# Order of the closing work: a stage's last operations, the copy-out of an accumulator and a gate's product, in a fused long-convolution and feed-forward kernel

## The chip, the cores and the metric

The kernel runs on one core of one Trainium2 chip. Its time is the device time of one execution in microseconds (us). Three runs of the kernel before gave 3606.44, 3606.97 and 3608.32 us; the median, 3606.97 us, is the number to compare with. All data are float32.

A core has five engines with a queue of instructions each, which they work off in order: TensorE (PE in the profile) for matmuls, VectorE (DVE), ScalarE (ACT), GpSimd (POOL), and SyncE (SP), which issues the transfers. Results of matmuls land in eight PSUM banks of 128 x 512 values, and a bank can be written again only when the engines that read it are done.

## The reference

Two blocks follow each other. The first is a long convolution along the sequence, by FFT, gated on both sides; its output, 49,920 rows of 128 values, is the input of a feed-forward block whose gate is a cosine.

```python
h_filt = (np.maximum(pos_emb @ w1, 0.0) @ w2) * np.exp(-0.01 * pos)[:, None]
u = x * v                                     # (4, 12480, 128)
y = irfft(rfft(u, n=2*S, axis=1) * rfft(h_filt, n=2*S, axis=0), n=2*S, axis=1)[:, :S]
a = (x * y).reshape(49920, 128)
h = a @ w_in                                  # 128 -> 2048
out = (h * np.cos(h)) @ w_out                 # 2048 -> 128
```

## The kernel before

**The convolution** is a two-level transform made of matmuls, one sequence (batch) b of the four after the other. Its stages are generators: `u_units` (multiply x and v, and fold), `f1_units` and `f2_units` (forward transform, and in the second the product with the filter's spectrum), `i1_units` and `i2_units` (inverse). Each of them is a call of `units` (L609), which cuts the n units of a stage into `parts` chunks each and yields after every chunk, with a number: what the chunk is worth in steps of the feed-forward block. Within a chunk it issues the matmuls of unit j, one piece of `after(j-1)` (what takes the previous unit out of PSUM) and one piece of the loads ahead. When the last unit's chunks are through, its own `after` is still to come: L632 issues all of it without a yield, and L634 yields `REST`, 3.0.

`after` has these pieces: in `u_units` two products of x and v (L441) and one pair of sums (L451); in `f1_units` one copy (L471); in `f2_units` four, each with one product of a PSUM bank and the spectrum on VectorE (L516, L518), every second one with a sum on GpSimd (L519); in `i1_units` two (a ScalarE copy and two VectorE sums, L563, L565); in `i2_units` the gating product (L591), after which `made` counts a finished group of 104 rows.

`inverse_units` (L815) runs `i2_units` of batch b and, between its chunks, the `u_units` of batch b+1, then the rest of these alone; it multiplies the chunk's worth of the `i2` by 3.5/1.5 (b = 0) or 3.4/1.5.

**The feed-forward block** takes blocks of 128 rows x 4 positions (512 tokens), n = 0 to 97, and each in 16 steps c of 128 of the 2048 hidden columns. A loop (L1203) with a running number i issues one step per turn, in this order:

1. `moe_down` of step i-7 (`LAG` = 7): 12 matmuls into the accumulator `acca` or 16 into `accb` (L911), in pairs of steps. On the block's last two steps `moe_evict` copies the accumulators out into `ot`: after pc = 14 L925 and L926 read `acca`; after pc = 15 the VectorE operations L929, L931 and L932 read `accb`. Because of the lag this falls on c = 5 and c = 6 of the next block. After pc = 15 comes one call of `convolve` (L1210).
2. `moe_up` of step i: four matmuls into a bank `ph` (L139), then L879 on ScalarE and L880 on VectorE, which bring the phase into one turn.
3. `act(i-1)`: `moe_act` of the step before, the sine on ScalarE (L885) and the product gate = h * cos(h) on VectorE (L886), the last reader of that step's bank.
4. `moe_sums` of the pair that began at i-4, on GpSimd (L894, L897, L898), which the later `moe_down` reads.
5. `convolve` (L1253), unless the next step is one with pc = 15 (`later`, L1251): then the chunk waits for step 1 of the next turn and stands behind the copy-out.

`convolve` (L1155) adds 1.0 to `owed` and takes chunks until their worth has used it up. Where rows are needed that no chunk has made yet, `load` (L1135) takes chunks without counting, and `hurry` (L1140) does so some steps earlier, up to the end of a stage, which it knows by a yield equal to `REST`.

`phase_bank` (L869) takes the bank of a step's phase from a pool of three (`ph`); once the convolution is through (`made` = 120) odd steps use the three banks (`cv`) that the convolution had. `accb` and `acca` have one bank each.

Ahead of the loop the filter's and the first sequence's transform run without the feed-forward block, with the same `units`.

Of the kernel before, what the change touches and what calls it, by code (L numbers as in the profile page):

```python
# [34 lines left out]
def kernel(  # L35
# [48 lines left out]
    B, S, D = x.shape  # L84
# [3 lines left out]
    R = S // N2  # L88
# [15 lines left out]
    NFC = DFF // P  # L104
    G = BANK // D
    UA = 2
    NG = N2 // G
# [3 lines left out]
    LAG = 7  # L111
# [487 lines left out]
        yield  # L599

    rows_psum = []
    made = [0]
    ot_tiles = []
    zbs = {}

# [3 lines left out]
    def units(n, steps, before, mm, after, parts, ahead=2, skip=0):  # L609


        for j in range(min(ahead, n)):
            for _ in before(j) or ():
                pass
        yield 0.0
        last = iter(())
        for j in range(n):
            early = iter(before(j + ahead) or () if j + ahead < n else ())
            now = None
            for i in range(parts):  # L620
                if i == skip or 2 * (i - skip) == max(parts, 2):
                    now = mm(j, now, int(i > skip))
                if i == 0 and parts == 1:
                    now = mm(j, now, 1)
                next(last, None)
                next(early, None)
                yield steps / parts
            for _ in early:
                pass
            next(last, None)  # L630
            last = after(j, now)
        for _ in last:  # L632
            pass
        yield REST  # L634

    SOME = range(2, NG, 5)
    REST = 3.0
# [207 lines left out]
    def first_row(n):  # L845
        return min(R + (n - 1) * P, NROWS) if n else 0
# [36 lines left out]

    def moe_act(ph, part, scale):
        nc.scalar.activation(part, part, AF.Sin, scale=scale)  # L885
        nc.vector.tensor_tensor(part, ph, part, op=ALU.mult)  # L886

    def moe_sums(pool, n, gt):
# [74 lines left out]
    with tc.manual_schedule():  # L963
        with tc.tile_pool(name="psum", bufs=8, space=PSUM) as psum, \
# [8 lines left out]
            parts = slots[:, :, 0:2 * N1, :].rearrange("p b (r k) i -> p r k b i", r=2)  # L973
# [158 lines left out]
        conv = convolutions()  # L1132
# [6 lines left out]

        def hurry(n):  # L1140

            while made[0] * R < first_row(n + 1):
                if next(conv) == REST:
                    return

        while made[0] == 0:
            next(conv)
# [3 lines left out]
        steps = [(n, c) for n in range(NALL) for c in range(NFC)]  # L1151
        hidden, pairs, gates, ots, obs = {}, {}, {}, {}, {}
        due, turned, taken = False, -3, {}

        def convolve():  # L1155
            nonlocal owed
# [7 lines left out]

            return taken[i] and not (taken[i - 1] and taken[i - 2])

        def act(i):
            if i in hidden:
                moe_act(*hidden.pop(i))

        def turns(n):

# [30 lines left out]
        for i in range(len(steps) + LAG):  # L1203
            if i >= LAG:
                pn, pc = steps[i - LAG]
                moe_down(pn, pc // 2, pc % 2, *gates[i - LAG - pc % 2])
                if pc >= NFC - 2:
                    ots[pn] = moe_evict(mpool, pn, pc % 2, ots.get(pn))
                if pc == NFC - 1:
                    convolve()  # L1210
            rest, early = iter(()), False
            if i < len(steps):
                n, c = steps[i]
                if c == 0:
                    due = 0 < n < SINGLE or n % 2
                if n == 0 and c == NFC // 2:
                    load(1)
                soon = n + 2 <= SINGLE or n % 2 == 0
                if c == (NFC - 5 if soon else SOON - 3) and 0 < n < NALL - 2:
                    hurry(n + 2)  # L1220
                if soon and c == (NFC - 2 if n else NFC - 1) and n + 2 < NALL:
                    load(n + 2)
                if n >= SINGLE and n % 2 and c == SOON and n + 2 < NALL:
                    load(n + 2)
                if n == 0 and c == NFC - 2:
                    pt = bank()
                    moe_turn(1, pt)
                    moe_turned(mpool, 1, pt)
                early = due and c >= AT
                if early:  # L1230
                    if n >= SINGLE:
                        act(i - 1)
                    convolve()
                    if n < SINGLE or c == AT + 3 or not just_taken(i):
                        due, turned = False, i
                        rest = turns(n)
                        next(rest)
                ph = phase_bank(c)
                next(rest, None)
                if c % 2 == 0:  # L1240
                    pairs[i] = mpool.tile([P, 2, BANK], F32, name="gt", bufs=4)
                hidden[i] = moe_up(mpool, n, c, pairs[i - c % 2], ph)
            for _ in rest:
                pass
            act(i - 1)
            if i - 4 in pairs:
                gates[i - 4] = moe_sums(mpool, steps[i - 4][0], pairs.pop(i - 4))
            if i == turned + 2:
                for k in sorted(obs):
                    moe_store(k, obs.pop(k))  # L1250
            later = i + 1 >= LAG and steps[i + 1 - LAG:][:1] and steps[i + 1 - LAG][1] == NFC - 1  # L1251
            if not early and not later:
                convolve()  # L1253
        for n in sorted(ots):
            moe_store(n, moe_rows(n, ots[n], moe_back(n, ots[n])))
# [28 lines left out]
```

## Time and profile before

| | |
|---|---|
| runs | 3606.44, 3606.97, 3608.32 us |
| profiled execution | 3609.1 us, of which the profile's span is 3607.3 us |
| mean granted TensorE clock | 0.999 |
| TensorE busy | 3554.6 us (99%) |
| VectorE busy | 2833.4 us (79%) |
| GpSimd busy | 2746.1 us (76%) |
| ScalarE busy | 2232.6 us (62%) |
| before the loop | to about 345 us of the span |
| convolution beside the feed-forward block | to about 2947 us |
| feed-forward block alone | from there to the end |

A row of the timeline gives the start, the duration, the engine, the line, the operation, what it writes and reads, and how many instructions were merged into it; in brackets stands how long the engine had been idle and what released it. A row of the stretches gives the length of the stretch and then each engine's busy time with its number of instructions, the granted clock of TensorE (1.00 is full speed), the share of time of the DMA engines and what they moved. A row of the waits says who waited for whom: total, times, longest. Matmuls overlap in the array, and their ends are modelled, so a short stop of TensorE can hide inside a "busy" duration; it shows between the starts of two rows.

### The profile page before, as it was taken

Reading aid. Unit: us, or ns where it says so; the run is one execution under the profiler, and the core shown is the slowest. Engines: PE = TensorE matmul, PEld = TensorE weight load, DVE = VectorE, ACT = ScalarE, POOL = GpSimd, SP = SyncE. Lnnn points to the kernel's source line nnn. Section 1 sums busy time; section 2 is a strip of 40 time slices with the busy share of each in tenths; the row PEclk is TensorE's granted clock in tenths of the full one; section 3 lists DMA queues with packets and bytes.
Section 4 is the critical chain, followed back from the end, with each engine's and each line's share of the span. In section 5 each row is a group of like instructions: output and inputs, shape, how many; then the busy total and the mean of one; then the engine's idle time right before and its main releaser. Section 6 shows DMA issues by size and latency. Waiting matters only on the chain.

```text
span 3607.3 us, 102214 instructions
## 1 busy us (share of the span) xinstructions
PE 3554.6 (99%) x40830; PEld 2549.7 (71%) x40830; DVE 2833.4 (79%) x5293; ACT 2232.6 (62%) x4482; POOL 2746.1 (76%) x3236
## 2 busy tenths in 40 slices
PE   8999999999999999999999999999999999999999
PEld 7996767666677777666677776766667876666666
DVE  7888885688887875688877786688887667877877
ACT  7776766656655556666655556665555456667666
POOL 7777985688856996688864897589884458888887
PEclk9999999999999999999999999999999999999999
DMA  7545540122214650022212661022220440000000
GB/s 191 157 147 169 159 117 13 34 72 72 70 32 127 173 139 17 24 76 72 75 30 60 172 171 51 13 64 70 75 63 20 132 125 25 16 22 25 16 22 17
DMA packets 224195, 281.84 MB, mean 78 GB/s; under 512 B 23386, under 2 KB 161122, under 8 KB 223594
## 3 DMA queue, kind: packets, MB, share of 16 engines
q1 hardware_dynamic: 223722, 275.30, 26.7%
q8 instruction: 325, 5.32, 0.6%
q14 instruction: 148, 1.21, 0.1%
HBM read 194.75 MB, written 80.46 MB: 76 GB/s over the span
## 4 chain that ended last, share of the span: by engine, by line
PE 82%; DVE 5%; POOL 2%; ACT 1%; issue 1%; DMA 1%; SPq 0%; ACTq 0%; DVEq 0%; POOLq 0%
PE ph L139 30%; PE accb L911 17%; PE cv L139 17%; PE acca L911 13%; PE cv L459 3%; DVE gt L886 2%; DVE gt L880 1%; PE cv L143 1%; PE ph L143 1%; ACT gt L879 1%; POOL ts L894 1%; DVE xt L441 0%; POOL ts L897 0%; DMA tm<-td 0%; DVE t L518 0%
## 5 line engine op out<-in xcount | busy, mean ns | idle before, releaser
L879 ACT ACTIVATE gt<-ph 128x512 int32<-128x512 f32 (+1 forms) x1376 | 822.0, 597 | 1138.6 <-PE ph L139 1100.0
L880 DVE SCALAR_TENSOR_TENSOR gt<-ph,gt 128x512 f32<-128x512 f32 (+1 forms) x1376 | 946.2, 688 | 658.7 <-ACT gt L879 654.9
L139 PE MATMUL ph<-at,w_in_sb 128*64 128x512 f32 (+2 forms) x5504 | 1424.8, 593 | 14.1 <-DVE gt L886 12.3
L894 POOL TENSOR_TENSOR ts<-gt 128x512 f32<-128x512 f32 (+2 forms) x784 | 999.7, 1275 | 568.0 <-PE accb L911 408.3
L885 ACT ACTIVATE gt<-gt 128x512 f32<-128x512 f32 (+1 forms) x1568 | 975.4, 622 | 26.9 <-DVE gt L880 25.9
L886 DVE TENSOR_TENSOR gt<-ph,gt 128x512 f32<-128x512 f32 (+1 forms) x1376 | 934.6, 679 | 8.8 <-ACT gt L885 7.7
L911 PEld LDWEIGHTS accb<-ts,w_out_sb 128*64 128x64 f32 x9408 | 571.2, 137 | 271.3 <-issue 222.3
L911 PE MATMUL accb<-ts,w_out_sb 128*64 128x128 f32 (+2 forms) x9408 | 653.1, 272 | 1.6 <-DVE ot_a L932 0.2
L898 POOL TENSOR_TENSOR ts<-gt,ts 128x256 f32<-128x256 f32 (+2 forms) x784 | 576.5, 735 | 61.4
L897 POOL TENSOR_TENSOR ts<-ts,gt 128x256 f32<-128x256 f32 (+2 forms) x784 | 575.5, 734 | 61.5
L911 PEld LDWEIGHTS acca<-gt,w_out_sb 128*64 128x64 f32 x6272 | 401.2, 136 | 247.3 <-issue 211.2
L911 PE MATMUL acca<-gt,w_out_sb 128*64 128x128 f32 (+2 forms) x6272 | 480.4, 272 | 0.0
L139 PEld LDWEIGHTS ph<-at,w_in_sb 128*64 128x64 f32 x5504 | 352.0, 137 | 39.9 <-issue 14.7
L911 PE MATMUL acca<-ts,w_out_sb 128*64 128x128 f32 (+1 forms) x3136 | 310.5, 273 | 1.8 <-POOL ts L897 1.4
L911 PE MATMUL accb<-gt,w_out_sb 128*64 128x128 f32 (+1 forms) x3136 | 310.8, 272 | 0.0
L139 PEld LDWEIGHTS cv<-slots,tm 96*40 96x40 f32 (+1 forms) x3840 | 226.1, 125 | 113.8 <-issue 107.7
L519 POOL TENSOR_TENSOR slots<-slots,t 120x256 f32<-120x256 f32 x288 | 210.2, 733 | 69.3 <-DVE t L518 65.8
L139 PE MATMUL cv<-slots,tm 96*40 96x128 f32 (+1 forms) x3840 | 253.8, 273 | 2.8 <-DVE slots L565 1.5
L911 PEld LDWEIGHTS acca<-ts,w_out_sb 128*64 128x64 f32 x3136 | 202.7, 137 | 4.7 <-POOL ts L897 4.3
L139 PEld LDWEIGHTS cv<-even,slots 120*33 120x33 f32 (+1 forms) x3072 | 165.9, 125 | 55.9 <-issue 48.6
L911 PEld LDWEIGHTS accb<-gt,w_out_sb 128*64 128x64 f32 x3136 | 205.0, 137 | 0.0
L139 PE MATMUL cv<-at,w_in_sb 128*64 128x512 f32 (+1 forms) x768 | 198.4, 587 | 0.0
(149 smaller groups left out, 3834.7 us busy)
## 6 DMA issues: line engine op xcount, KB each, us to landing
h<-hd SPq DMA_DIRECT2D x144, 240.0 KB
tm<-td SPq DMA_DIRECT2D x96, 312.0 KB
xt<-in_x_dram SPq DMA_DIRECT2D x120, 208.0 KB
xs<-in_x_dram SPq DMA_DIRECT2D x120, 208.0 KB
zd<-xs SPq DMA_DIRECT2D x119, 208.0 KB
at<-zd SPq DMA_DIRECT2D x96, 256.0 KB
vt<-in_v_dram SPq DMA_DIRECT2D x90, 208.0 KB
w<-wd SPq DMA_DIRECT2D x144, 105.0 KB
```

Of the source, the lines that this page charges most:

```text
L139: nc.tensor.matmul(dst[lo:hi], left[:, lo:hi], right, start=start, stop=stop, **how)
L143: nc.tensor.transpose(dst, src, ident[0:n, 0:n])
L459: nc.tensor.matmul(dst[lo:hi], u[:, b, lo:hi, i], c1[0:u.shape[0], r:r + 2, :].rearrange("p r k -> p (r k)"), start=True, stop=True)
L519: nc.gpsimd.tensor_tensor(y[:, r], y[:, r], t[:, r], op=op)
L879: nc.scalar.activation(turns, ph[:, 0:m], AF.Identity, bias=phase)
L880: nc.vector.scalar_tensor_tensor(out=part, in0=ph[:, 0:m], scalar=phase, in1=turns, op0=ALU.add, op1=ALU.subtract)
L885: nc.scalar.activation(part, part, AF.Sin, scale=scale)
L886: nc.vector.tensor_tensor(part, ph, part, op=ALU.mult)
L894: nc.gpsimd.tensor_tensor(ts[:, 0:2, 0:half], gt[:, :, half:2 * half], gt[:, 0, 0:2 * half].rearrange("p (h n) -> p h n", h=2), op=ALU.sub ...
L897: nc.gpsimd.tensor_tensor(t[2], t[1], b11, op=ALU.add)
L898: nc.gpsimd.tensor_tensor(t[3], b21, t[2], op=ALU.subtract)
L911: nc.tensor.matmul(acc[h * CB:(h + 1) * CB, place, 0:r], w_out_sb[:, pair, weight, :], right[:, h * r:(h + 1) * r], start=(pair == 0 and i ...
```

## The change

Four edits.

- `units`: the last unit's `after` is issued piece by piece with a yield after each, worth one chunk (`steps / parts`), and the closing yield is worth what is left of 3.0, but at least 2.0. A counter `ended` goes up at a stage's end.
- `hurry` recognizes a stage's end by `ended`.
- `moe_act` becomes a generator with a yield between the sine and the product; `act` can hand back the rest of it.
- In the loop `later` is replaced by `late`. It is true when the next step has pc = 15 and either the convolution is through or an `i2` of the batches 1 to 3 is under way (`made` over 30 and no multiple of 30). Only then the chunk stands behind the copy-out; and there the product L886 of the step before is held back too, and issued behind the copy-out, ahead of that chunk. At all other blocks the chunk keeps its place at the end of the step, ahead of the copy-out of `accb`.

```diff
-        for _ in last:
-            pass
-        yield REST
+        rest = REST
+        for _ in last:
+            yield steps / parts
+            rest -= steps / parts
+        ended[0] += 1
+        yield max(rest, 2.0)
...
         nc.scalar.activation(part, part, AF.Sin, scale=scale)
+        yield
         nc.vector.tensor_tensor(part, ph, part, op=ALU.mult)
...
-            while made[0] * R < first_row(n + 1):
-                if next(conv) == REST:
-                    return
+            done = ended[0]
+            while made[0] * R < first_row(n + 1) and ended[0] == done:
+                next(conv)
...
+        held, late = iter(()), False
...
-        def act(i):
+        def act(i, held=False):
             if i in hidden:
-                moe_act(*hidden.pop(i))
+                acts = moe_act(*hidden.pop(i))
+                next(acts)
+                if held:
+                    return acts
+                for _ in acts:
+                    pass
+            return iter(())
...
                     ots[pn] = moe_evict(mpool, pn, pc % 2, ots.get(pn))
-                if pc == NFC - 1:
+                for _ in held:
+                    pass
+                if late:
                     convolve()
...
-            act(i - 1)
+            last = 0 <= i + 1 - LAG < len(steps) and steps[i + 1 - LAG][1] == NFC - 1
+            late = last and NG < made[0] and (made[0] % NG or made[0] == B * NG)
+            held = act(i - 1, late)
...
-            later = i + 1 >= LAG and steps[i + 1 - LAG:][:1] and steps[i + 1 - LAG][1] == NFC - 1
-            if not early and not later:
+            if not early and not late:
                 convolve()
```

More of the change, by code (lines that the diff above doesn't have):

```diff
@@ L601 @@
     rows_psum = []
-    made = [0]
+    made, ended = [0], [0]
     ot_tiles = []
```

## The prediction

> **What bounds the kernel now.** I read the page first, then busy time by stage, then the timeline at the places that the diff touches.
>
> ```profile
> PE 3554.6 (99%) x40830; PEld 2549.7 (71%) x40830; DVE 2833.4 (79%) x5293; ACT 2232.6 (62%) x4482; POOL 2746.1 (76%) x3236
> PE 82%; DVE 5%; POOL 2%; ACT 1%; issue 1%; DMA 1%; SPq 0%; ACTq 0%; DVEq 0%; POOLq 0%
> ```
>
> ```profile
> 686.00:1013.00 327.00, 324.58 (x3444) 211.70 (x3442) 285.35 (x566) 197.75 (x362) 287.81 (x341) 1.00 0.23 68
> 2947.00:3585.00 638.00, 636.79 (x6970) 425.19 (x6966) 510.43 (x848) 444.34 (x822) 515.31 (x565) 1.00 0.07 20
> ```
>
> The second line of the page is the chain that ended last; the two stretches are an `f2` stage and the part in which the feed-forward block is alone. TensorE sets the time: 99% busy, 82% of the chain. The change adds and removes no matmul, so it can only move the short stops of TensorE. Those are read between the starts of matmul rows. The last stage in its regular course, then at a copy-out:
>
> ```profile
> 3121.27 1.03 PE L139 MATMUL cv<-at,w_in_sb 128*64 128x512 f32 x4
> 3122.13 0.82 PE L911 MATMUL accb<-ts,w_out_sb 128*64 128x128 f32 x12
> 3122.78 0.39 PE L911 MATMUL accb<-gt,w_out_sb 128*64 128x128 f32 x4
> ...
> 3124.51 1.03 PE L139 MATMUL cv<-at,w_in_sb 128*64 128x512 f32 x4
> 3125.60 0.88 PE L911 MATMUL accb<-ts,w_out_sb 128*64 128x128 f32 x12
> ```
>
> ```profile
> 3123.06 0.68 DVE L880 SCALAR_TENSOR_TENSOR gt<-cv,gt 128x512 f32<-128x512 f32 x1
> 3123.65 0.68 DVE L886 TENSOR_TENSOR gt<-ph,gt 128x512 f32<-128x512 f32 x1
> 3124.25 0.42 DVE L929 TENSOR_TENSOR ot_b<-accb,ot_b 128x256 f32<-128x256 f32 x1
> ...
> 3125.03 0.42 DVE L932 TENSOR_TENSOR ot_b<-accb,ot_b 128x256 f32<-128x256 f32 x1
> ```
>
> From the phase's four matmuls to `accb` it is 0.86 us in the regular course and 1.09 at the copy-out: `accb` starts 0.15 us after L932 ends (3125.45), so the bank was late by 0.23. The old accumulator had been complete since 3123.17; VectorE was busy with L880 and then with the product L886, which stood ahead.
>
> **The last stage (held product).** The weight loads show the same wait with a count (from 2950 to 3595 us):
>
> ```profile
> PEld accb L911 <- PE cv L139: 21.6, 24, 0.9
> ```
>
> 24 times, one per copy-out. With L886 behind the copy-out, L929 can follow L880 at about 3123.65 instead of 3124.25, 0.60 earlier, which covers 0.23 with 0.37 to spare. Removed: 24 x 0.21 to 0.23, say **5.0 us**. What L886 loses: its bank is next but two in a pool of three and not wanted for steps; its pair's second product, on which GpSimd's sums wait, keeps its place, since VectorE does the same work up to there. Late next is nothing for 0.37 us. The cost of holding is therefore put at 0; at worst the stop stays, so this term lies between 0 and -5.5.
>
> **The end of `u` in the first sequence.** Here TensorE stands longest inside the loop.
>
> ```profile
> 523.30 0.48 DVE L428 MEMSET slots<- 104x512 f32 x1
> 523.39 1.08 PE L139 MATMUL ph<-at,w_in_sb 128*64 128x512 f32 x4
> 523.71 1.22 DVE L441 TENSOR_TENSOR xt<-xt,vt 104x256 f32<-104x256 f32 x2
> 524.96 2.38 DVE L451 TENSOR_TENSOR slots<-xt 104x256 f32<-104x256 f32 x2
> 527.87 0.67 DVE L886 TENSOR_TENSOR gt<-ph,gt 128x512 f32<-128x512 f32 x1
> ...
> 528.69 1.69 PE L139 MATMUL ph<-at,w_in_sb 128*64 128x512 f32 x4 [3.55 <-DVE gt L886]
> ```
>
> ```profile
> 529.00:532.50 3.50, 3.50 (x26) 2.66 (x24) 2.03 (x4) 1.12 (x2) 1.12 (x3) 0.51 0.74 215
> ```
>
> The burst (memset, two products, two sums) holds VectorE for 4.0 us, 523.30 to 527.3, and L880 and L886 behind it then free a phase bank. A regular step is 1.62 us (3121.27 to 3124.51 are two), so TensorE wanted the bank at 525.0 and got it 3.7 us later. After that the granted clock is 0.51 for 3.5 us, another 1.7 us of work lost. After the change the memset, each product and the pair of sums come from different chunks, two or one per step. The stop is 0.3 us shorter than its burst, and some 0.4 of it VectorE owed already (L441 of the unit before had run long beside GpSimd), so a burst B by itself should leave about B - 0.7. For the pair of sums B is between 0.7 and 2.4, by this row and the one above:
>
> ```profile
> L441 DVE TENSOR_TENSOR xt<-xt,vt x91: 356/873/2836, 295.1 to 2196.5; 104x256 f32<-104x256 f32 x91
> ```
>
> (Shortest, median, longest in ns.) I take twice the median, 1.74, and again 0.4 owed from the steps before, which hold the products: a stop of 1.74 - 0.7 + 0.4 = 1.4 instead of 3.7, 2.3 saved (1.3 to 3.5). The clock's 1.7 goes entirely if a stop of that size leaves the clock alone; the trace shows stops of 1.1 us (below) at full clock and this one of 3.55 followed by half, so I take it gone and keep it as a bound. Term: **-4.0** (-1.3 to -5.2).
>
> The Trainium skill, "TensorE: Matmul & The Clock Gate", section "Part 1: The HAM clock gate", puts the threshold at an idle window of about 3.4 us; by it a stop of 1.4 or even 2.4 us stays at full clock, and a remaining stop would have to be over 3.4 us for this part of the term to vanish. A rule against this edit stands in "SBUF — State Buffer", section "Who interferes with whom": a VectorE instruction with two SBUF inputs and a GpSimd instruction that reads SBUF exclude each other for the whole instruction. The row of L441 agrees (356 ns at best, 2836 at worst). By it each of three separated pieces may wait for GpSimd anew; at median less shortest, 0.52 us each, that is an estimate of 1.6 us given back, and the sum below would be -11.6.
>
> **The ends of `f2`** (three in the loop). Four VectorE operations come at once:
>
> ```profile
> 1829.31 0.42 DVE L516 TENSOR_TENSOR slots<-cv,h 120x256 f32<-120x256 f32 x1
> ...
> 1830.30 0.42 DVE L518 TENSOR_TENSOR t<-cv,h 120x256 f32<-120x256 f32 x1
> ...
> 1832.06 1.08 PE L139 MATMUL ph<-at,w_in_sb 128*64 128x512 f32 x4 [1.12 <-DVE gt L886]
> ```
>
> ```profile
> 2686.30 1.08 PE L139 MATMUL ph<-at,w_in_sb 128*64 128x512 f32 x4 [0.79 <-DVE gt L886]
> ```
>
> Their 1.4 us delays a phase bank by 1.12 and 0.79 us; the first of the three ends I put at their mean, 0.96, together 2.9. Spread over four chunks they have the density of the stage itself, where single stops of 0.2 us remain. Term: **-2.5** (0 to -3.5).
>
> **The chunk ahead of the copy-out again, outside the last stage.** In `i1` the old place hurts:
>
> ```profile
> 1872.20 1.02 PE L139 MATMUL cv<-even,slots 120*64 120x120 f32 x16
> ...
> 1875.41 1.43 PE L139 MATMUL cv<-even,slots 120*64 120x120 f32 x24
> 1876.64 1.06 PE L139 MATMUL ph<-at,w_in_sb 128*64 128x512 f32 x4
> 1877.50 0.61 PE L139 MATMUL cv<-even,slots 120*64 120x120 f32 x8
> 1878.58 0.61 PE L139 MATMUL cv<-even,slots 120*64 120x120 f32 x8 [0.46 <-DVE slots L565]
> ```
>
> ```profile
> 1051.16 0.61 PE L139 MATMUL cv<-even,slots 120*64 120x120 f32 x8 [0.47 <-ACT gt L885]
> ```
>
> ```profile
> 2779.03 0.61 PE L139 MATMUL cv<-even,slots 120*64 120x120 f32 x8 [0.48 <-DVE slots L565]
> ```
>
> Eight matmuls take 1.43 - 1.02 = 0.41, so the last eight should start at 1877.91; they start 0.67 later, because two helpings stand close together with the copy-out between their VectorE sums. Five copy-outs fall into `i1`, the first and the last with the two rows of 0.47 and 0.48. With the chunk back in its step the sums come first and banks free evenly. Term: **-2.8** (0 to -3.3).
>
> In `f2`, where 11 copy-outs fall into each stage, the chunk's product goes ahead of the copy-out instead of behind it (the stretch's columns here are L932's alone, with its count):
>
> ```profile
> 686.00:1013.00 327.00, 4.67 (x11) 1.00 0.23 68
> ```
>
> ```profile
> 880.82 0.42 DVE L932 TENSOR_TENSOR ot_a<-accb,ot_a 128x256 f32<-128x256 f32 x1
> 881.16 0.42 DVE L516 TENSOR_TENSOR slots<-cv,h 120x256 f32<-120x256 f32 x1
> ...
> 881.71 0.82 PE L911 MATMUL accb<-ts,w_out_sb 128*64 128x128 f32 x12
> ```
>
> `accb` starts 0.47 after L932's end and needs 0.15: 0.32 to spare, against L516's 0.34. Where the chunk brings two products it is late by some 0.35. But L886, which TensorE waits for right afterwards, has the same operations ahead of it in either order, so such a wait mostly replaces one. I take **+1.0** for `f2`, and +0.6 for copy-outs beside `u` and the first `i2`, whose chunks bring longer operations: **+1.6** (0 to +27, the upper end below).
>
> **More credit per stage.** An `f2` end now yields 4 x 0.85 + 2.0 instead of 3.0, a `u` end 3 x 0.67 + 2.0: some 3 steps later per sequence. The rows are taken by `load` and `hurry` all the same; this run of matmuls shows what it costs (chain in order of time):
>
> ```profile
> 1063.93 35.73 PE cv L139 x686
> ```
>
> 343 pairs at 0.104 us, against 0.41/4 = 0.103: TensorE is at its rate there, so a longer run costs nothing. If that cover failed, 9 steps x 1.6 = 14 us. Ahead of the loop, TensorE waits for the first tables of `f2`:
>
> ```profile
> 136.75 1.10 PE L492 MATMUL ps<-ftile,w 124*120 124x256 f32 x4 [0.94 <-DVE w L332]
> ```
>
> Their making is tied to a count of chunks from the end of the conversion of the weights, and the extra yields of `f1` let it start before that stage's last chunk: **-0.5** (0 to -0.9).
>
> **Sum:** -5.0 - 4.0 - 2.5 - 2.8 + 1.6 - 0.5 = -13.2. The profiled execution took 3609.1 us (span 3607.3), 2.1 over the median: 3595.9 there, 3606.97 - 13.2 = **3594 us** for the median.
>
> **Rivals.**
>
> - **Only the last stage gains.** Freed time at the stage ends is spent waiting for what is late next: `f2` has VectorE at 285.35 of 327 us, 87%, and GpSimd at 88%. The last stage has no such partner. 3607 - 5 = 3602, chance 0.22.
> - **The copy-outs lose outside the last stage: slower.** Thirty-three fall into `f2`, seven beside `u` and the first `i2`. If each pays two of a chunk's products, 0.68 us, in place of the 1.6 above, that is 27 us: 3594 - 1.6 + 27 = 3619; with one, 0.34 us or 14, it is 3606. It decides where the copy-out ends less than 0.15 + 0.34 us ahead of `accb`, and 0.47 is on the edge. For it speaks VectorE's 87% in the stage, against it the wait that is only replaced. Chance 0.12, of which 0.09 at the full price.
> - **More falls away**, stops of 0.2 to 0.5 us through `f2` included, because the phase against the blocks shifts: 3587, chance 0.08.
> - That the condition never holds would leave the 24 stops in place; `made` does reach 120 and the odd steps' `cv` banks above show it, so this has no chance of its own.
>
> The forecast has 0.58. A difference under 0.2%, 7.2 us, is about what a measurement here can tell from none: faster than 3599.8 is 0.58 + 0.08 = 0.66, the same 0.22 + 0.03 = 0.25, slower 0.09. The forecast's own range is 3589 to 3600; with the second case it reaches 3603, and 3588 below, which leaves out the slower case and most of the fourth, some 0.18.
>
> **What would show it.** After the change the 24 waits of the weight loads of `accb` are gone and L929 follows L880 in the last stage; no stretch near 530 us has a clock near 0.5 and the stop there is under 2.4 us; L516 and L518 stand apart at an `f2` end; no [0.4x <-DVE slots L565] stands behind a copy-out in `i1`. I am wrong if `accb` in `f2` starts right behind L932 with no shorter wait of `ph` after it, or if the half clock comes back.

## The result and the profile after

Seven runs of the changed kernel took 3594.92 to 3597.2 us, median **3595.82 us**; seven of the kernel before on the same chip 3606.44 to 3609.01, median 3607.2. The ratio is 0.9968, 95% interval 0.9956 to 0.9979. The profiled execution after took 3597.2 us (span 3595.4, clock 0.999), beside 3609.1 (span 3607.3) before.

The page after, the lines that answer to those shown of before:

```profile
span 3595.4 us, 102297 instructions
...
PE 3552.1 (99%) x40830; PEld 2533.6 (70%) x40830; DVE 2835.3 (79%) x5293; ACT 2228.1 (62%) x4482; POOL 2748.4 (76%) x3236
...
PE 86%; DVE 3%; POOL 1%; ACT 1%; issue 1%; DMA 0%; SPq 0%; ACTq 0%; POOLq 0%; DVEq 0%
```

The work is the same, instruction for instruction on TensorE; its share of the chain rose from 82 to 86% and VectorE's fell from 5 to 3%. In the kernel after, lines have moved: the phase is L883 (was L880), the product L890 (L886), the copy-out of `accb` L933, L935, L936 (L929, L931, L932), the matmuls into `acca` and `accb` L915 (L911), the sums L898, L901, L902.

Waits of TensorE beside the convolution (345 to 2947 us; who waits <- for whom: total, times, longest), before:

```profile
PE ph L139 <- DVE gt L886: 10.0, 18, 3.6
...
PE cv L139 <- DVE slots L565: 3.6, 9, 0.6
```

and after:

```profile
PE ph L139 <- DVE gt L890: 5.4, 11, 2.2
...
PE cv L139 <- DVE slots L565: 1.8, 5, 0.6
PE accb L915 <- DVE ot_a L936: 1.8, 3, 1.4
...
PE accb L915 <- DVE ot_b L936: 1.2, 4, 0.4
```

The phase's bank and the sums of `i1` are waited for half as long. In exchange seven waits for the copy-out of `accb` have come, 3.0 us in all, of which one is 1.4; the list of before has none.

**The last stage.** TensorE and VectorE at a copy-out, after:

```profile
3117.44 1.03 PE L139 MATMUL cv<-at,w_in_sb 128*64 128x512 f32 x4
3118.30 0.83 PE L915 MATMUL accb<-ts,w_out_sb 128*64 128x128 f32 x12
```

```profile
3115.98 0.68 DVE L883 SCALAR_TENSOR_TENSOR gt<-cv,gt 128x512 f32<-128x512 f32 x1
3116.58 0.41 DVE L933 TENSOR_TENSOR ot_b<-accb,ot_b 128x256 f32<-128x256 f32 x1
...
3117.36 0.42 DVE L936 TENSOR_TENSOR ot_b<-accb,ot_b 128x256 f32<-128x256 f32 x1
3117.70 0.68 DVE L890 TENSOR_TENSOR gt<-ph,gt 128x512 f32<-128x512 f32 x1
```

L933 follows L883, the product L890 comes last, and from the phase to `accb` it is 0.86 us (3117.44 to 3118.30), the regular course, where it was 1.09. In the weight loads from 2945 to 3585 us no line of `accb` waiting for a matmul is left; first of that list stands

```profile
PEld accb L915 <- issue: 105.9, 375, 0.4
```

The gain can be read from the copy-outs' own starts. The last operation of every second copy-out (those into `ot_a`; times, shortest/median/longest ns, first and last start), before and after:

```profile
L932 DVE TENSOR_TENSOR ot_a<-accb,ot_a x12: 424/424/426, 2987.7 to 3585.1; 128x256 f32<-128x256 f32 x12
```

```profile
L936 DVE TENSOR_TENSOR ot_a<-accb,ot_a x12: 424/424/425, 2981.4 to 3573.0; 128x256 f32<-128x256 f32 x12
```

22 blocks lie between the first and the last: 597.4 us before, 591.6 after, 0.26 less per block, 6.3 for the 24.

**The end of the first `u`.** VectorE, and the matmuls that wait for it:

```profile
522.71 0.42 DVE L441 TENSOR_TENSOR xt<-xt,vt 104x256 f32<-104x256 f32 x1
...
524.72 1.41 DVE L441 TENSOR_TENSOR xt<-xt,vt 104x256 f32<-104x256 f32 x1
...
527.25 0.56 DVE L441 TENSOR_TENSOR xt<-xt,vt 104x256 f32<-104x256 f32 x1
527.85 2.24 DVE L451 TENSOR_TENSOR slots<-xt 104x256 f32<-104x256 f32 x2
```

```profile
524.95 1.08 PE L139 MATMUL ph<-at,w_in_sb 128*64 128x512 f32 x4 [0.27 <-DVE gt L890]
...
527.48 1.08 PE L139 MATMUL ph<-at,w_in_sb 128*64 128x512 f32 x4 [0.58 <-DVE gt L890]
...
531.43 1.97 PE L139 MATMUL ph<-at,w_in_sb 128*64 128x512 f32 x4 [2.22 <-DVE gt L890]
```

```profile
524.00:526.00 2.00, 1.73 (x21) 1.00 (x18) 2.00 (x3) 1.12 (x2) 1.92 (x3) 1.00 0.00 0
...
530.00:532.00 2.00, 0.57 (x2) 0.32 (x4) 2.00 (x5) 0.63 (x1) 0.67 (x1) 0.87 0.24 60
532.00:534.00 2.00, 2.00 (x10) 1.11 (x8) 0.48 (x1) 0.56 (x2) 0.00 (x0) 0.50 0.77 209
534.00:536.00 2.00, 2.00 (x25) 1.69 (x23) 1.29 (x2) 0.55 (x2) 0.42 (x1) 0.78 0.70 227
```

The last product and the pair of sums come in one step: no L883 or L890 stands between 527.25 and the sums' end at 530.09. The one stop of 3.55 us has become three of 0.27, 0.58 and 2.22, and behind the last the clock is half again (0.50 from 532 to 534; the shares below 1.00 on either side make it some 3.4 us). A stop that was not there before has come a little earlier, where a product of an earlier unit of the same stage stands ahead of a copy-out:

```profile
508.01 1.36 DVE L441 TENSOR_TENSOR xt<-xt,vt 104x256 f32<-104x256 f32 x1
```

```profile
510.64 0.88 PE L915 MATMUL accb<-ts,w_out_sb 128*64 128x128 f32 x12 [1.41 <-DVE ot_a L936]
```

This stop needs both edits. With the loop's edit alone and with the chunk ahead everywhere (both below) no product of `u` falls into this step. With the stage ends' edit alone the product stands behind the copy-out; there it took 0.41 us (at 508.49), and the longest stop near it is 0.34.

So the place on which the prediction put its second largest term gave nothing in this execution, and the total was right all the same. The experiments look for what made it up. The theory with which they began: the held product pays in the last stage, the chunk's order in `i1`, and a spread end only where its pieces fit into what VectorE has to spare. Its rivals: the longer pauses at the stage ends do it, or holding is free and good at every copy-out.

A number used from here on: the **stops** of TensorE, by how much the interval between the starts of two successive matmuls exceeds the interval that their shapes need, summed over a stage from the trace's rows. From 345 us to the end they fall by some 13 us (12.6 to 14.2, by how small an excess is still counted), so they are read only as differences. The execution's time fell by 11.9; what lies ahead took 1.0 longer (first `i2` matmul at 277.3 us, 276.3 before). Two kernels with the same order differ by up to about 1 us in a single stage.

### The profile page after: what moved, and what is told of

Read it like the earlier page. It is cut to its first block, busy times and chain, and to the rows that moved or that the text cites. A ratio compares the mean times of both kernels' runs of the same rounds, so it can differ in the third digit from the quotient of the medians.

```text
span 3595.4 us, 102297 instructions
## 1 busy us (share of the span) xinstructions
PE 3552.1 (99%) x40830; PEld 2533.6 (70%) x40830; DVE 2835.3 (79%) x5293; ACT 2228.1 (62%) x4482; POOL 2748.4 (76%) x3236
## 4 chain that ended last, share of the span: by engine, by line
PE 86%; DVE 3%; POOL 1%; ACT 1%; issue 1%; DMA 0%; SPq 0%; ACTq 0%; POOLq 0%; DVEq 0%
PE ph L139 31%; PE accb L915 18%; PE cv L139 18%; PE acca L915 13%; PE cv L459 3%; PE cv L143 1%; PE ph L143 1%; DVE gt L890 1%; DVE gt L883 1%; ACT gt L882 1%; DVE xt L441 0%; POOL ts L898 0%; POOL ts L901 0%; POOL slots L451 0%; POOL ts L902 0%
## 5 line engine op out<-in xcount | busy, mean ns | idle before, releaser
L883 DVE SCALAR_TENSOR_TENSOR gt<-ph,gt 128x512 f32<-128x512 f32 (+1 forms) x1376 | 946.0, 687 | 645.4 <-ACT gt L882 640.4
L898 POOL TENSOR_TENSOR ts<-gt 128x512 f32<-128x512 f32 (+2 forms) x784 | 1000.7, 1276 | 556.3 <-PE accb L915 384.9
L890 DVE TENSOR_TENSOR gt<-ph,gt 128x512 f32<-128x512 f32 (+1 forms) x1376 | 934.0, 679 | 6.7 <-ACT gt L888 5.6
L915 PEld LDWEIGHTS accb<-ts,w_out_sb 128*64 128x64 f32 x9408 | 563.8, 136 | 258.8 <-issue 218.9
L915 PE MATMUL accb<-ts,w_out_sb 128*64 128x128 f32 (+2 forms) x9408 | 648.8, 272 | 3.5 <-DVE ot_a L936 1.8
L902 POOL TENSOR_TENSOR ts<-gt,ts 128x256 f32<-128x256 f32 (+2 forms) x784 | 577.3, 736 | 61.5
L901 POOL TENSOR_TENSOR ts<-ts,gt 128x256 f32<-128x256 f32 (+2 forms) x784 | 575.0, 733 | 61.5
L915 PEld LDWEIGHTS acca<-gt,w_out_sb 128*64 128x64 f32 x6272 | 393.5, 136 | 256.7 <-issue 219.5
L915 PE MATMUL acca<-gt,w_out_sb 128*64 128x128 f32 (+2 forms) x6272 | 476.3, 272 | 0.0
L139 PEld LDWEIGHTS ph<-at,w_in_sb 128*64 128x64 f32 x5504 | 345.2, 137 | 33.5 <-issue 11.9
L915 PE MATMUL acca<-ts,w_out_sb 128*64 128x128 f32 (+1 forms) x3136 | 306.1, 272 | 2.1 <-POOL ts L901 1.9
L139 PEld LDWEIGHTS cv<-slots,tm 96*64 96x64 f32 (+1 forms) x3840 | 226.0, 125 | 114.6 <-issue 109.9
L915 PE MATMUL accb<-gt,w_out_sb 128*64 128x128 f32 (+1 forms) x3136 | 306.7, 272 | 0.0
L139 PE MATMUL cv<-slots,tm 96*64 96x128 f32 (+1 forms) x3840 | 253.3, 273 | 1.8 <-DVE slots L565 1.5
L139 PEld LDWEIGHTS cv<-even,slots 120*64 120x64 f32 (+1 forms) x3072 | 164.7, 125 | 54.6 <-issue 50.6
L915 PEld LDWEIGHTS acca<-ts,w_out_sb 128*64 128x64 f32 x3136 | 199.1, 137 | 3.6 <-POOL ts L901 3.4
L915 PEld LDWEIGHTS accb<-gt,w_out_sb 128*64 128x64 f32 x3136 | 200.9, 137 | 0.0
```

The source lines that it names most:

```text
L139: nc.tensor.matmul(dst[lo:hi], left[:, lo:hi], right, start=start, stop=stop, **how)
L883: nc.vector.scalar_tensor_tensor(out=part, in0=ph[:, 0:m], scalar=phase, in1=turns, op0=ALU.add, op1=ALU.subtract)
L898: nc.gpsimd.tensor_tensor(ts[:, 0:2, 0:half], gt[:, :, half:2 * half], gt[:, 0, 0:2 * half].rearrange("p (h n) -> p h n", h=2), op=ALU.sub ...
L901: nc.gpsimd.tensor_tensor(t[2], t[1], b11, op=ALU.add)
L902: nc.gpsimd.tensor_tensor(t[3], b21, t[2], op=ALU.subtract)
L915: nc.tensor.matmul(acc[h * CB:(h + 1) * CB, place, 0:r], w_out_sb[:, pair, weight, :], right[:, h * r:(h + 1) * r], start=(pair == 0 and i ...
```

## The experiments

Each was timed in five rounds against the kernel before (median 3607.11 to 3607.6 us beside them). The first four split the change, the next five turn its single choices, the last three look for something better.

**The loop alone** (after, with `units` and `hurry` as before) and **the stage ends alone** (before, with the new `units` and `hurry`).

```diff
# loop alone
-        rest = REST
         for _ in last:
-            yield steps / parts
-            rest -= steps / parts
-        ended[0] += 1
-        yield max(rest, 2.0)
+            pass
+        yield REST
# ends alone: the same lines the other way round, in the kernel before
```

> The loop's edit alone (product held, copy-out and chunk reordered), stage ends as before. Theory, local stops add up: last stage -6.1 us (two blocks take 54.0 instead of 54.5 us in the changed kernel's trace, 24 blocks), i1 -2.5, copy-outs behind a chunk in f2, u and the first i2 +0 to +1.6: 3607 - 7.5 = 3599 to 3600. Rival, the order in the loop gives everything and the stage ends nothing: 3596. Rival, only the last stage counts and the rest is given back: 3601 to 3602.

> The stage ends' edit alone (closing pieces spread, end counted), loop as before. Theory: the four pieces of f2 no longer come at once (-1 to -2.5 over three ends), the u end of the first sequence -0.2 to -2, the half clock there stays or goes (-0 to -1.7): 3607 - 4 = 3603, between 3601 and 3606. Rival, the loop gives everything: 3607. Rival, the ends carry half of the gain as predicted (4.0 + 2.5 + 0.5 = 7.0): 3600.

Loop alone: 3600.16 us (ratio 0.9982, 0.9973 to 0.9990), -7.0. Ends alone: 3604.02 (0.9991, 0.9982 to 1.0000), -3.1. Together they would be -10.1; the change is -11.4.

**Two halves of the loop's edit**, both with `units` and `hurry` as before: the product held in the last stage only and the chunk behind the copy-out at every block, as it was; and the chunk ahead of the copy-out everywhere, nothing held.

```diff
# last stage held
+            late = last
+            held = act(i - 1, last and made[0] == B * NG)
# chunk first
+            late = False
```

> Kernel before, with nothing but the product held behind the copy-out while the feed-forward block is alone; the chunk waits for the copy-out everywhere as before. Theory: 24 stops of 0.21 to 0.26 us go, -5.0 to -6.2: 3601 to 3602, and nothing else in the trace moves. Rival, the chunk's place has a share in the last stage's gain (or the stop moves to the next phase bank): under -2, 3605 or more.

> Kernel before, with the chunk at the end of its step at every block, ahead of the copy-out, no product held, stage ends as before. Theory: five stops of 0.6 us in i1 fall to 0.1 (-2.5), f2 waits for accb where it waited for a phase bank (0 to +1), the first i2 and the u stages lose 0.5 to 2, i2 of later sequences lose 0 to 1: 3607 - 1, between 3604 and 3609. Rival, the copy-outs outside the last stage lose (0.68 us at each of 40): 3630; at 0.34 each: 3618.

Last stage held: 3600.58 us (0.9983, 0.9974 to 0.9992), -6.5. Its copy-outs into `ot_a` in the last stage:

```profile
L933 DVE TENSOR_TENSOR ot_a<-accb,ot_a x12: 424/425/425, 2985.1 to 3576.6; 128x256 f32<-128x256 f32 x12
```

591.5 us for the 22 blocks, as in the kernel after: the gain of that stage belongs to the held product alone. Chunk first: 3604.72 us (0.9993, 0.9984 to 1.0002), -2.4; the interval reaches 1, so the time by itself does not tell this from no change, and the stops have to speak for it. The old wait of the weight loads is still there in the last stage:

```profile
PEld accb L912 <- PE cv L139: 21.5, 24, 0.9
```

Its stops fall by 2.6 us in the three `i1` (0.6, 1.0, 1.0). In the three `f2` they fall by 0.8, no more than the scatter named above; counted with other limits for small excesses it is nothing. The two halves make -8.9, but the loop alone gave -7.0: something in that edit costs about 2 us, and the halves leave out just one part of it, the late chunk with a held product beside the `i2` of the later sequences.

**The late chunk by its place.** Once also beside the first `i2`, and once in the last stage alone:

```diff
# also the first i2
+            late = last and (made[0] % NG or made[0] == B * NG)
# last stage alone
+            late = last and made[0] == B * NG
```

> The changed kernel, with the chunk behind the copy-out and the product held also beside the i2 of the first sequence. Theory: the stop of 1.57 us near 509 us, where a 1.4 us product of u stands ahead of the copy-out, goes; the other four copy-outs there stay near: 3596 - 1.5 = 3594 to 3595. Rival, the place of the chunk is indifferent there since the next phase bank is as late: 3596.

> The changed kernel, with the chunk behind the copy-out and the product held only while the feed-forward block is alone; beside the i2 of later sequences the chunk comes first as elsewhere. Theory: i2 of later sequences has 1.6 to 4 us of room ahead of accb, so either order costs the same: 3596, within 1. Rival, from the sum of single edits (chunk first alone -2.4, held product in the last stage alone -6.5, both with the i2 exception only -7.0): the exception costs 2 us: 3594.

Also the first `i2`: 3595.55 us (0.9968, 0.9955 to 0.9980), no difference. It does not settle the stop near 509 for which it was made: `made` is 30 at that copy-out, so the chunk keeps its place there, and the trace has L441 ahead of the copy-out (1.32 us at 507.21) and a stop of 1.36 as before. Last stage alone: 3593.93 (0.9964, 0.9952 to 0.9977), 1.9 below the kernel after, though single runs of the two overlap (3592.81 to 3596.98 here). The stops beside the `i2` of the second and third sequence, over all kernels here: 4.4 to 6.0 us in the seven with the late chunk and the held product there (4.9 after, 6.0 loop alone), 3.6 to 4.0 in the four with the chunk ahead and nothing held, and 3.7, 5.0 and 5.4 in the three with the chunk behind and nothing held (last stage held, before, ends alone). So the pair of late chunk and held product costs 1 to 2 us there. How much of it is the chunk's and how much the hold's is not separated: of the three with the chunk behind and nothing held, one stops no longer than those with the chunk ahead.

**The product held at every copy-out**, also where a phase has only three banks.

```diff
-            held = act(i - 1, late)
+            held = act(i - 1, last)
```

> The changed kernel, with the product held behind the copy-out at every block, the chunk's place as in the changed kernel. Theory: f2's waits for accb (0.2 to 0.3 us, nine of them in three stages) go, but the phase bank that TensorE waits for next is freed by the held product and its follower at the same time as before, so the wait moves back to it: 0 to -1.5, 3594.5 to 3596. Rival, the waits for accb are a cost of their own: -3 to -5, 3591 to 3593. Rival, the held product frees its phase bank too late (0.6 us at 40 blocks): over 3600.

3624.84 us (1.0048, 1.0034 to 1.0061), 29.0 above the kernel after. Waits over the same stretch of the loop:

```profile
PE ph L139 <- DVE gt L890: 39.4, 46, 3.3
```

35 more waits than the 11 above, for the phase's bank each time, 0.97 us on the mean; 33 copy-outs lie in `f2`. There the held product is the last reader of the bank that the next phase but one takes, and VectorE has to get through the copy-out first.

**The pair of sums at the first `u`'s end on GpSimd**, like all the others; the memset goes there with it.

```diff
-            yield from u_units(b, u, engine, place, 1, lambda j: 2 * (
-                nc.vector if b == 1 and j == H // UA - 1 else nc.gpsimd,))
+            yield from u_units(b, u, engine, place, 1, lambda j: 2 * (nc.gpsimd,))
```

> The changed kernel, with the last sums and the memset of the first sequence's u on GpSimd as for the other sequences, so that VectorE has no burst at the end of u. Theory: the stop of 2.4 us near 529 and the half clock of 3.4 us after it go (-2.4 - 1.7), f1 may wait for GpSimd's sums (0 to +2): 3596 - 3 = 3592 to 3594. Rival, GpSimd, 92% busy there, passes the delay on to the gates' sums and to f1: 3596 or more. On the clock: by an idle window of about 3.4 us the stop of 2.4 could not have halved it, so that it would stay halved without the stop; by a share of work in a fixed window it goes.

3592.42 us (0.9959, 0.9947 to 0.9972), 3.4 below the kernel after and with no run in common (3591.92 to 3593.21). The stretch of the old stop:

```profile
520.00:535.00 15.00, 14.88 (x161) 11.11 (x158) 11.30 (x19) 9.11 (x18) 13.90 (x17) 1.00 0.24 68
```

TensorE busy 14.88 of 15 us, at full clock: VectorE's pair of sums (with the memset) was what held it. GpSimd takes it on at 13.90 of 15 us.

**Four more steps of credit at every stage's end.**

```diff
-        yield max(rest, 2.0)
+        yield max(rest, 2.0) + 4.0
```

> The changed kernel, with every stage's closing yield worth 4.0 more, so that each sequence's transforms lag the feed-forward block by some 16 steps more and more of them are taken uncounted. Theory of the prediction: that run of matmuls goes at TensorE's rate, so the credit is free as long as it falls into i1: 3596, within 2. Rival: each step of credit costs a step, 16 steps or 26 us per sequence: over 3650. A middle way: the uncounted run reaches back into f2, where VectorE (87% busy beside the feed-forward block) cannot follow matmuls taken alone: 3600 to 3615.

3605.5 us (0.9995, 0.9986 to 1.0004), 9.7 above the kernel after. New or grown among the waits beside the convolution:

```profile
PE acca L915 <- POOL ts L901: 4.8, 4, 1.6
PE accb L915 <- DVE ot_a L936: 3.4, 6, 1.4
PE cv L139 <- POOL slots L519: 3.1, 1, 3.1
```

In the kernel after the first of these is 0.9 (two times), the second 1.8 (three times), and the third is not there. The end of the `u` beside the second sequence shows how, GpSimd and then TensorE:

```profile
1358.18 1.43 POOL L451 TENSOR_TENSOR slots<-xt 104x256 f32<-104x256 f32 x2
...
1363.72 1.44 POOL L451 TENSOR_TENSOR slots<-xt 104x256 f32<-104x256 f32 x2
1365.10 0.93 POOL L441 TENSOR_TENSOR xt<-xt,vt 104x256 f32<-104x256 f32 x1
1365.99 1.27 POOL L898 TENSOR_TENSOR ts<-gt 128x512 f32<-128x512 f32 x1
```

```profile
1368.12 0.44 PE L915 MATMUL acca<-ts,w_out_sb 128*64 128x128 f32 x4 [1.61 <-POOL ts L901]
```

For 27 us ahead of 1358 GpSimd has no operation of `u`; then three units' operations come within 12 us, between the sums of the feed-forward pairs, and `acca` waits for these. The third line of the waits is the first matmul of `i1` standing 3.1 us for the last sum of `f2`, which had just been issued; behind it the clock is at 0.50 for 6.8 us. What was put off has to be made up where rows are due, and there the chunks follow each other without the gaps that VectorE and GpSimd need. Stops grow at the later `u` ends by 5.7 us and at the `f2` ends by 4.2 (3.9, 1.7, 2.1 instead of 1.3, 1.1, 1.1), in `f2` by 3.5; in `f1` and `i1` they shrink by about 3.5.

**Wider gaps within the same end.** Every closing piece yields 2.0 instead of `steps / parts`.

```diff
         for _ in last:
-            yield steps / parts
-            rest -= steps / parts
+            yield 2.0
+            rest -= 2.0
```

> The changed kernel, with each closing piece worth 2.0 steps instead of one chunk (0.4 to 0.85), so that VectorE has two steps between two pieces. Theory: at the end of the first u the stops of 0.4 and 0.7 us ahead of the long one go since nothing is owed from piece to piece, the stop of 2.4 falls to 1.5 to 1.9 as forecast, and the f2 ends lose their waits for accb (0.3 to 0.6 each): 3596 - 2 to -3, 3593 to 3594. Rival, the end of u is bound by VectorE's and GpSimd's work as a whole, whatever the spacing: 3596.

3593.34 us (0.9963, 0.9949 to 0.9977), 2.5 below the kernel after. At the first `u` (500 to 560 us) the bank is waited for

```profile
PE ph L139 <- DVE gt L890: 1.1, 3, 0.6
```

against 3.6 us, five times, the longest 2.2, in the kernel after. The `f2` ends have stops of 0.7, 0.5 and 0.7. The later `u` ends, where the pieces lie on GpSimd, have 1.7 and 2.3 instead of 1.1 each.

This run also limits what the one before it shows. By the yields, the wider gaps put off 4.0 steps more at a `u` end (3 x 2.0 + 2.0 instead of 3 x 0.67 + 2.0), 1.0 at an `f1`, 4.6 at an `f2` and 3.0 at an `i1` end: 12.6 per sequence where the credit run put off 16 at these four. Yet it is 2.5 us faster and not 9.7 slower. So the loss does not go by the credit alone; whether its place (behind a stage instead of between its last pieces) or the last few steps bring it was not tested.

**Together.** The sums on GpSimd and the late chunk in the last stage alone; and these two with the wider gaps.

> The changed kernel with both edits that were faster by themselves: sums at the end of the first u on GpSimd, and the chunk ahead of the copy-out beside every i2. Theory, the two touch different places and add up: 3596 - 3.4 - 1.9 = 3590.5. Rival, part of each was the half clock, which can go only once: 3592.

> The three edits that each brought 2 to 3 us over the kernel after, in one: the chunk ahead of the copy-out everywhere and the product held only in the feed-forward block alone, the pair of sums at the end of the first u on GpSimd, and the closing pieces worth 2.0 steps each instead of steps / parts. If the wider spacing does more than the u end (its f2 ends had 0.5 to 0.73 us of stops each instead of 1.1 to 1.25), the gain adds: 3590.7 - 1.5 = 3589.2 us. If it brought its 2.5 us only at the end of the first u, where the burst is gone already, 3590.7 us. If the wider spacing pushes the chunks against the rows that are due, as the four steps of extra credit did (the later u ends then have 1.7 and 2.3 us of stops instead of 1.1), it is slower than without: 3592.5 us.

The first: **3590.7 us** (0.9955, 0.9942 to 0.9967; 3590.43 to 3590.96), below every execution of its two parts. The second: 3591.16 (0.9954, 0.9941 to 0.9968), the same: the wider gaps pay where a burst lies on VectorE, and that one was gone. 3590.7 us is 16.5 below the kernel before and 5.1 below the kernel after.

## Why the prediction was right, and where it was right by cancellation

Forecast 3594, measured 3595.8; the sum for the profiled execution was -13.2, its time fell by 11.9. Term by term:

| term | predicted | stops, spans and runs |
|---|---|---|
| held product, last stage | -5.0 (0 to -5.5) | -6.3 by the copy-outs' starts, -6.5 run by itself |
| end of the first `u` | -4.0 (-1.3 to -5.2) | +1.8 in stops: -0.3 at the end itself, the rest ahead of it, most of all at 510.64; half clock still there in the profiled execution |
| three `f2` ends | -2.5 (0 to -3.5) | -0.3 |
| `i1`, chunk ahead | -2.8 (0 to -3.3) | -2.6 run by itself |
| chunk ahead elsewhere | +1.6 (0 to +27) | about 0 (-0.8) in `f2`, run by itself; with the stage ends' edit the stop at 510.64, counted above |
| late chunk and hold beside `i2` | not priced | +1 to +2 |
| credit | 0 (up to 14) | not measured apart; 4 steps more per stage cost 9.7, 12.6 more per sequence as gaps did not |
| first tables | -0.5 (0 to -0.9) | -0.3 in that wait (0.94 is 0.68), but the first `i2` matmul comes no earlier: 277.3 us, 276.3 before, 275.8 to 277.3 over all kernels |
| later `u` ends, `f2` as the phase shifts | not in the sum | -1.1 and about -3 |

- **Last stage: right, undersized.** The stop is gone, and nothing became late next. It gave 0.26 us per copy-out instead of 0.21 to 0.23 and so passed the bound of 5.5. The mark read was the one longer interval ahead of `accb`; where the other 0.03 per block lay isn't shown.
- **The end of the first `u`: failed.** The step that failed is "a burst B by itself should leave about B - 0.7", with 1.74 us for the pair of sums and 0.4 owed. The pair was not by itself and was longer: the last product stood in the same step, so B was 2.8 us (527.25 to 530.09) instead of 1.74. B - 0.7 is then 2.1, and the stop was 2.22. The product a step earlier took 1.41. VectorE was busy without a break from 524 to 532: a regular step of 1.62 us leaves it some 0.4 beside L883 and L890 (0.6 each from start to start), and pieces of 0.56 to 2.24 us, one or two to a step, do not fit into that, so what each was late was handed on to the next. Spacing them by one chunk changed the shape of the stop and hardly its sum. Giving them room (two steps each) took 2.1 us off the stops there, and taking the largest off VectorE 4.3.
- The estimate of 1.6 us given back, for which the prediction named the Trainium skill's "SBUF — State Buffer", section "Who interferes with whom", points the right way: the spread L441 took 1.36 and 1.41 us beside a busy GpSimd, 0.42 at best in the same stretch (at 522.71), and the stop of 1.41 at 510.64 is one of them at work. GpSimd beside the one at 508.01, and (its column alone) during the ones at 522.71 and 524.72:

```profile
507.81 1.29 POOL L898 TENSOR_TENSOR ts<-gt 128x512 f32<-128x512 f32 x1
```

```profile
522.71:523.13 0.42, 0.00 (x0) 1.00 0.00 0
524.72:526.13 1.41, 1.33 (x2) 1.00 0.00 0
```

  GpSimd stood still during the short one. The one at 508.01 ended at 509.37, 0.27 us after GpSimd's operation (509.10). Those at 524.72 and 527.25 ended 0.28 us after one (525.85 and 526.13, 527.53 and 527.81). That is what waiting for the whole operation looks like.
- **The half clock: the size that was taken as safe is wrong.** The prediction took it gone with a stop of 1.4 us, and with any under 3.4. Behind a stop of 2.22 us it came back in the profiled execution, which the prediction had named as a sign of being wrong. In the kernel with the late chunk in the last stage alone, the same stop did not bring it:

```profile
530.75 1.08 PE L139 MATMUL ph<-at,w_in_sb 128*64 128x512 f32 x4 [2.23 <-DVE gt L890]
```

  So the length of the stop alone does not decide. The Trainium skill, "TensorE: Matmul & The Clock Gate", "Part 1: The HAM clock gate", speaks of a free-running window of about 3.4 us, and the traces agree. The prediction took the same figure as the length that a stop must reach, and the row at 531.43 contradicts that. In eight of the fourteen the clock falls inside the loop, and always a whole number of 3.413 us after its first rise to full: 152 of them in six kernels, 146 with the product held everywhere, 303 with more credit. On this grid, the window that holds the stop and the next one, first in the kernel after, then in the other:

```profile
528.06:531.47 3.41, 1.19 (x18) 0.72 (x15) 3.41 (x5) 1.23 (x2) 2.45 (x3) 1.00 0.07 13
531.47:534.88 3.41, 3.41 (x17) 2.19 (x19) 1.82 (x4) 1.11 (x2) 0.00 (x0) 0.50 0.72 206
```

```profile
527.02:530.43 3.41, 1.50 (x16) 0.78 (x12) 3.38 (x5) 0.99 (x2) 2.81 (x3) 1.00 0.00 0
530.43:533.84 3.41, 3.09 (x32) 2.27 (x34) 2.66 (x5) 1.35 (x3) 0.62 (x1) 1.00 0.70 189
```

  In the first TensorE is idle for 2.22 of the 3.41 us, in the second for 1.91, because its stop reaches over the border. In all fourteen traces the windows of the loop with 2.22 us of idle time or more (eight) are followed by half clock and those with 1.91 or less by none. At the programs' ends the clock falls behind windows with less idle time too (1.5 us at the least), so idle time is not the exact measure; no run moved a stop on purpose. Of the 1.7 us, a part was saved in some executions: the mean clock rounds to 1.0 in five of the seven after, and in 10 of the 66 of the kernel before beside the experiments.
- **The `f2` ends: failed.** "Spread over four chunks they have the density of the stage itself" was so, and at the second end the stop for the phase's bank is 0.28 instead of 1.27; but in two of the three ends a copy-out now falls between the pieces, and L518 stands ahead of it, as the chunk's new order has it:

```profile
1833.76 0.41 DVE L518 TENSOR_TENSOR t<-cv,h 120x256 f32<-120x256 f32 x1
1834.09 0.41 DVE L933 TENSOR_TENSOR ot_b<-accb,ot_b 128x256 f32<-128x256 f32 x1
```

```profile
1835.44 0.77 PE L915 MATMUL accb<-ts,w_out_sb 128*64 128x128 f32 x10 [0.43 <-DVE ot_b L936]
```

```profile
2685.79 0.88 PE L915 MATMUL accb<-ts,w_out_sb 128*64 128x128 f32 x12 [0.44 <-DVE ot_b L936]
```

  A wait for `accb` of 0.43 and 0.44 us stands there now. The prediction had worked out this price, a copy-out late by some 0.35 with a chunk's products ahead of it, and applied it only to the middle of the stage. The 0.96 us that it put down for the first of the three ends stands in no row of before either: between 1003 and 1024 us none shows a matmul waiting for a phase's bank.
- **`i1`: right.** Run by itself the chunk ahead of the copy-out took 2.6 us off; in the kernel after, `i1` and its borders lost 3.9, the rest from its different start.
- **The copy-outs elsewhere: no cost in `f2`, and the slower rival fell.** In `f2` of the third sequence (2355 to 2680 us) the kernel after has one wait for a copy-out:

```profile
PE accb L915 <- DVE ot_b L936: 0.2, 1, 0.2
```

  and the kernel before (2360 to 2680) three for the phase's bank:

```profile
PE ph L139 <- DVE gt L886: 0.9, 3, 0.4
```

  The argument that such a wait replaces one of L886 held, and by itself the chunk's order cost nothing there. Beside the first `u`, where the prediction allowed 0.6 us in all for the longer operations of its chunks, the one stop at 510.64 cost 1.4. The rival that asked 0.34 us of each of 40 copy-outs had the margin right and the replacement wrong.
- **"The cost of holding is put at 0"** was worked out for six banks and then used for the `i2` as well, where a phase has three. At three banks and a full VectorE (`f2`) it costs 0.97 us a time; beside `i2` it costs, with the late chunk, 1 to 2 us in all. The condition in the change spares the first of these and not the second.
- **"A longer run costs nothing"** looked at TensorE alone. It held for the matmuls of `i1`, whose stops shrank; in the credit run the price is paid at the ends of `u` and `f2`, by GpSimd and VectorE. What the 3 steps of the change itself cost was not measured apart, and the run with wider gaps shows that more steps can go unpaid.
- **Only the last stage gains** (0.22) fell: the ends and the chunk's order by themselves gave 3.1 and 2.4 us (each interval reaches 1.000), and the whole change gave 4.9 more than the last stage by itself.

The failures amount to +5.8 at the first `u`, +2.2 at the `f2` ends, 1 to 2 beside `i2`, and 1.0 ahead of the loop; on the other side stand 1.3 more in the last stage, 1.1 in `i1` and its borders, 1.6 to 2.4 less cost elsewhere, and about 4 that no term held. That these balance is luck: the two terms that held, the last stage and `i1`, give 9 of the 12 us, and the rest of the sum came near for reasons that it did not contain. A part of the unforeseen gain in `f2` comes with the stage ends alone (2.8 us of stops, 1.8 of it in the third `f2`) and moves from kernel to kernel with where blocks fall against stages, as the rival "More falls away" had it, if for much less than its 3587; no single cause of it was found.

## What to carry to other kernels

Before spreading a burst, compare each piece with what the engine has to spare per step: pieces larger than that hand their lateness on, and only wider gaps or another engine help. A last reader may be held back as far as its buffer's pool is deep, so price the hold separately at every depth that the kernel has. Work put off without a count can come back in a rush, and the rush must be priced on the slow engines and not on the fast one.

## What the hardware showed that was not expected

A TensorE stop of 2.22 us was followed by some 3.4 us at half clock (0.50), and one of 2.23 us at nearly the same place of another kernel by none (1.00), as the rows above show; what differed was how much of the stop lay in one window of 3.413 us (2.22 and 1.91 us). The time of one and the same VectorE product of two SBUF operands, L441, was 0.42 us at 522.71 and 1.41 at 524.72, 1.2 steps on, with GpSimd still during the first and busy for 1.33 us of the second.
